# Slots of routed tiles in fewer matmuls, one load of queries moved up, and the last tokens placed by float32 products

## The chip, the core and the metric

The kernel runs on one core of a Trainium2 chip. The metric is the time of one execution in microseconds of device time (us). Five engines work side by side, each through its own instructions in order: TensorE (PE; its weight loads are shown as PEld), VectorE (DVE), ScalarE (ACT), GpSimd (POOL) and SyncE (SP). They wait for each other by semaphores. Most DMA transfers are issued from SP's queue, the scattered and gathered rows from POOL's.

## The reference

Three layers in a row: an attention with a window of 32 and 32 global tokens, a layer of eight experts of which each token takes one, and a dense layer with a fixed curve. Cut to what matters:

```python
s_g = scale * q_g @ k_all.T;  out_g = softmax(s_g) @ v_all            # 32 global queries a head
s_l = concat(scale * q_l @ k_g.T, where(|i-j| <= 32, scale * q_l @ k_l.T, -1e9))
out_l = softmax(s_l) @ concat(v_g, v_l)                               # 512 local queries a head
x = tokens(out)                                                       # 1088 rows of 512

logits = x @ w_gate;  e = argmax(logits)
for i in range(N):                            # in the order of the tokens
    if counts[e[i]] < capacity:
        disp[e[i], counts[e[i]]] = x[i];  counts[e[i]] += 1
y = relu(disp @ w1) @ w2;  x = gate * y[e, pos]

h = x @ w_in;  out = where(h >= 1, h, where(h <= -1, 0, (h + 1)**2 / 4)) @ w_out
```

The shapes are 2 batches, 8 heads, 512 local and 32 global tokens, head size 64; 8 experts of 512 x 1024 and 1024 x 512; a dense layer of 512 x 2048 and 2048 x 512. The capacity given is 288 rows for each expert.

## The kernel before

**Attention.** The order is written out by hand as 16 steps: a step is one batch, one half of its 512 local queries (two tiles of 128) and one pair of heads. `scores` multiplies queries and keys (PE), DVE adds the mask and takes the maxima, `exps` is ACT's, `transp` turns the probabilities (PE), `evac_t` copies them out, `av` multiplies with the values. In the loop over the steps k, `exps(k + 1)` and `scores(k + 2)` come first, then what the table `first[k]` holds, then `transp(k)`, `evac_t(k)`, `av(k - 1)`, and then what `plan[k]` holds. The tables hold the global queries (`glob1`, `glob1b`, `glob2`, `glob3`, for four heads at a time, starting at steps 0, 3, 5 and 8), the filling with zeros of the expert buffers `xd` in DRAM, and the routing. From step 2 the weights of expert 0 are loaded too (`raw`), rounded by ACT (`H`, line 218), and their remainder is taken by POOL (`L`, line 230).

**Queries of the global tokens.** `load_unit(u)` and `load_values(u)` issue the loads of keys, queries and values of a pair of heads on SP; for every second u `load_values` also issues the load of four heads' global queries, `QG[u // 2]`, tile `qgt`. `glob1(6)`, in step 8, reads the last of them.

**Routing.** `route(k, b, tp)` is called for three groups of tiles: three tiles of batch 0 (steps 7 to 9), two (10 to 12), three tiles of batch 1 (13 to 15); the last two tiles, (1, 3) and (1, 4), follow behind the loop. For a group, `logits` and `choose` find the expert of each token as a one-hot tile `OH`. `slots` finds where each token goes: with matmuls of 8 columns it adds the experts' base addresses (`base_b`), the counts so far (`racc`), the counts of earlier tiles of the group (`ones_b`) and those of earlier tokens of the same tile (`tri_b`) in `pc`; DVE picks the token's own column (`ex`, `sidx`) and brings `racc` up to date. `x_rows` turns the attention output into rows of tokens (`px` on PE, `xr` on DVE, or on ACT for the 32 global tokens), and `scatter` writes them into `xd` with a DMA from POOL.

**Hand-over.** The first 128 rows of expert 0 are not read back once all tokens are in DRAM. `xt0` is loaded when the third tile of batch 1, (1, 2), has been scattered (line 714). The tokens of the two last tiles are added on PE: `place` (line 725) is a one-hot tile that says to which of the 128 rows each of their tokens goes, and `px0` sums `xt0` by the identity and the last tokens' rows by `place`. In before the last rows are split into two parts of a rounded type, `late0h`, `late1h` (ACT, line 723) and `late0l`, `late1l` (DVE, line 729), so that there are five groups of four matmuls. ACT and DVE then round `px0` into `X0` (lines 743 and 744), with which the first expert starts (line 842).

**Warming.** `keep_warm(n)` issues n matmuls of zeros, which nobody reads: 9 at the start, and 5, 3 and 2 around the hand-over.

**Experts and dense layer.** Eight experts follow, while ACT and DVE round the next weights; then the dense layer, in four groups of columns, over three chunks of tokens.

Of the kernel before, what the change touches and what calls it, by code (L numbers as in the profile page):

```python
# [8 lines left out]
F32 = mybir.dt.float32  # L9
F32R = mybir.dt.float32r  # L10
BF16 = mybir.dt.bfloat16
# [3 lines left out]
ALU = mybir.AluOpType  # L15
AX = mybir.AxisListType
ENG = mybir.EngineType

P = 128
WARM_0, WARM_1, WARM_2, WARM_3, WARM_4 = 9, 5, 3, 2, 0  # L20
WIN = 224


# [5 lines left out]
def tile_attention_moe_ffn(  # L29
# [23 lines left out]
    nc = tc.nc  # L53
    w_in, w_out = w_in.bitcast(U32), w_out.bitcast(U32)
    B, NHP = qd.shape[0], qd.shape[1]
    SL = qd.shape[3]
    EXT = kd.shape[3]
    SG = qg.shape[3] // 4
    D = 64
    S = SL + SG  # L60
    DM, NT = out.shape
    E, _, F = w1.shape
    DFF = w_out.shape[0]
    KD = DM // P
# [62 lines left out]
    def load_values(u):  # L127
        b, hp = divmod(u, NHP)
        VT[u] = at.tile([P, 5, P], F32, tag="vt", name=f"vt{u}", bufs=NBU)
        nc.sync.dma_start(VT[u], vx[b, hp])  # L130
        if hp % 2 == 1:
            QG[u // 2] = at.tile([P, 4 * SG], F32, tag="qgt", name=f"qgt{u}", bufs=4)
            nc.sync.dma_start(QG[u // 2], qg[b, hp // 2])

    mask_sb = at.tile([P, NLT, WIN], F32, name="mask_sb")
    load_unit(0, 0)
# [303 lines left out]
    def tile_rows(i):  # L440
        return SG if i == 0 else P
# [98 lines left out]
    def slots(b, lo, hi):  # L540

        pc = ps_v(f"pc{b}{lo}")
        n = hi - lo
        for i in range(lo, hi):
            o = pc[:, E * (i - lo):E * (i - lo + 1)]
            r = tile_rows(i)
            nc.tensor.matmul(o, ones_b[:1], base_b[:1], start=True, stop=False)
            nc.tensor.matmul(o, ones_b, racc, start=False, stop=False)
            for j in range(lo, i):
                nc.tensor.matmul(o, ones_b[:tile_rows(j)], OH[b][:tile_rows(j), j, :], start=False, stop=False)  # L550
            nc.tensor.matmul(o, tri_b[:r], OH[b][:r, i, :], start=False, stop=True)
        ts = slice(b * NB_ + lo, b * NB_ + hi)
        ex = rt.tile([P, NB_, E], F32, tag="ex", name=f"ex{b}{lo}", bufs=1)
        nc.vector.tensor_tensor(
            out=ex[:, :n, :], in0=pc[:, :E * n].rearrange("p (i e) -> p i e", e=E), in1=OH[b][:, lo:hi, :],
            op=ALU.mult)
        rs = rt.tile([P, E], F32, tag="rs", name=f"rs{b}{lo}", bufs=1)
        nc.vector.tensor_reduce(out=rs, in_=OH[b][:, lo:hi, :].rearrange("p i e -> p e i"), op=ALU.add, axis=AX.X)
        with nc.allow_low_precision(reason="whole numbers, one of the terms not zero"):
            nc.vector.tensor_reduce(out=sidx[:, ts], in_=ex[:, :n, :], op=ALU.add, axis=AX.X)  # L560
        nc.vector.tensor_tensor(out=racc, in0=racc, in1=rs, op=ALU.add)

    def scatter(b, i):
# [59 lines left out]
            nc.sync.dma_start(yd[0:1, :], zero[:1, :])  # L623


    def keep_warm(n):
        warm = ps_a("warm")
        for _ in range(n):
            nc.tensor.matmul(warm, zero.bitcast(BF16)[:, :P], zero.bitcast(BF16)[:, :512], start=True, stop=True)

    keep_warm(WARM_0)
    scores(0)
    exps(0)
    scores(1)
# [6 lines left out]
    load_values(4)  # L641
    load_unit(5)
    load_values(5)
    wq = [(u, c) for u in range(2) for c in range(4)]
    wn = 0

# [12 lines left out]
    def route(k, b, tp):  # L659

        lo, hi = (0, 3) if tp == 0 else (3, 5)
        i = 2 * tp + 1
        x = [lambda j=j: x_rows(b, j) for j in range(lo, hi)]
        sc = [lambda j=j: scatter(b, j) for j in range(lo, hi)]
        first[k] += [lambda: logits(b, i, 2), lambda: recips(b, i, i + 2)]
        plan[k] += [lambda: logits_t(b, i, 2)]
        if tp == 0:
            first[k].append(lambda: logits(b, 0, 1))
            plan[k].append(lambda: logits_t(b, 0, 1))
        plan[k] += [lambda: choose(b, lo, hi)]  # L670
        first[k + 1] += x[:1]
        plan[k + 1] += [lambda: slots(b, lo, hi)] + x[1:2] + sc[:1]
        plan[k + 2] += x[2:] + sc[1:]

    route(7, 0, 0)
    route(10, 0, 1)
# [41 lines left out]
    keep_warm(WARM_1)  # L718
    slots(1, 3, NB_)
    late = [XR[1, 3], XR[1, 4]]  # L720
    halves = [[rt.tile([P, DM], F32R, name=f"late{i}{n}") for n in "hl"] for i in range(2)]
    for (xa, _), x in zip(halves, late):
        nc.scalar.copy(xa, x)
    place = rt.tile([P, 2, P], F32R, name="place")
    nc.vector.tensor_tensor(
        out=place, in0=iota_sb.unsqueeze(1).to_broadcast([P, 2, P]),
        in1=sidx[:, ntile - 2:].unsqueeze(2).to_broadcast([P, 2, P]), op=ALU.is_equal)
    for (xa, xb), x in zip(halves, late):
        nc.vector.tensor_tensor(out=xb, in0=x, in1=xa.bitcast(F32), op=ALU.subtract)
    px0 = ps_t("px0")  # L730
    keep_warm(WARM_2)
    parts = [(halves[i][0], place[:, i, :]) for i in range(2)] + [(xt0, ident)]
    parts += [(halves[i][1], place[:, i, :]) for i in range(2)]
    for ns, k0 in ((range(5), range(KD)),):
        for n in ns:
            x, at_ = parts[n]
            for k in k0:
                ks = slice(k * P, (k + 1) * P)
                nc.tensor.matmul(px0[:, ks], x[:, ks], at_, start=n == k == 0, stop=n == 4 and k == KD - 1)
    keep_warm(WARM_3)  # L740
    v = px0.rearrange("p (k t) -> p k t", k=KD)
    for k0 in (slice(0, 2), slice(2, 4)):
# [668 lines left out]
```

## Time and profile before

| | |
|---|---|
| median of 3 runs | 465.1 us (462.73 to 465.33) |
| profiled execution, its own time | 462.71 us |
| its span | 460.8 us |
| granted clock of TensorE, mean | 1.00 |
| busy: PE, DVE, ACT, POOL | 442.3, 335.2, 242.9, 95.8 us |

The span is the time from the first to the last instruction of the profiled execution; 1.9 us lie around it. Times of single instructions are from that execution, which is 2.4 us below the median. In a timeline the number in brackets is how long the engine had been idle before the row, and what ended it.

### The profile page before, as it was taken

How to read it: one execution, taken by the hardware profiler on the slowest of the kernel's cores; microseconds unless marked ns; L12 is line 12 of the kernel's file. 1: busy time of each engine (PE TensorE's matmuls, PEld its weight loads, DVE VectorE, ACT ScalarE, POOL GpSimd, SP SyncE). 2: the span in 40 equal slices, each digit the busy share in tenths (PEclk: the TensorE clock that was granted, in tenths of full speed). 3: DMA queues.
4: the chain of work that ended last, by engine and by line, in shares of the span. 5: the costliest groups of instructions: out<-in, count | busy, mean ns of one | idle time of the engine just before them, and what ended most of it. 6: DMA issues, size and time to landing. Idle time of an engine off the chain costs nothing. (4 is left out here: it accounts for less than half of the span.)

```text
span 460.8 us, 8110 instructions
## 1 busy us (share of the span) xinstructions
PE 442.3 (96%) x2875; PEld 372.1 (81%) x2876; DVE 335.2 (73%) x715; ACT 242.9 (53%) x508; POOL 95.8 (21%) x98
## 2 busy tenths in 40 slices
PE   8998989999999999999999899998999999999997
PEld 4876677787577777777777799998999899999996
DVE  4787798674156389936898976787888988878633
ACT  5779666273244478726766675645444344534321
POOL 1105365300000000000001642232133131322321
PEclk9999999999999999999999999999999999999999
DMA  8999554589349169963986340653221410000203
GB/s 273 312 332 366 171 185 134 192 278 395 129 127 316 47 242 389 375 239 123 341 299 243 98 149 0 211 200 93 91 75 64 134 49 1 0 2 0 70 1 127
DMA packets 34595, 79.17 MB, mean 172 GB/s; under 512 B 3761, under 2 KB 8497, under 8 KB 34546
## 3 DMA queue, kind: packets, MB, share of 16 engines
q1 hardware_dynamic: 31698, 70.40, 44.8%
q0 software_dynamic: 1408, 4.46, 2.9%
q10 hardware_dynamic: 1440, 3.67, 2.3%
q8 instruction: 29, 0.48, 0.5%
q14 instruction: 20, 0.16, 0.1%
HBM read 63.77 MB, written 14.75 MB: 170 GB/s over the span
## 5 line engine op out<-in xcount | busy, mean ns | idle before, releaser
L1158 PE MATMUL fh<-oldH,H 128*128 128x256 f32 (+1 forms) x256 | 64.7, 328 | 2.6 <-DVE g L1176 2.1
L230 DVE TENSOR_TENSOR L<-raw,H 128x1024 fp32r<-128x1024 f32 x56 | 66.3, 1217 | 0.9 <-ACT H L218 0.6
L1198 PE MATMUL acc<-oldH,H 128*128 128x256 f32 (+2 forms) x240 | 65.1, 332 | 1.3 <-ACT H L280 0.7
L218 ACT CAST H<-raw 128x1024 fp32r<-128x1024 f32 x57 | 58.0, 1049 | 10.0 <-PEq L895 8.2
L1158 PEld LDWEIGHTS fh<-oldH,H 128*128 128x128 f32 x256 | 44.8, 189 | 6.0 <-DVE g L1176 2.5
L1184 ACT CAST oldH<-g 128x256 fp32r<-128x256 f32 (+2 forms) x36 | 17.9, 496 | 56.8 <-DVE g L1176 56.8
L1198 PE MATMUL acc<-oldH,L 128*128 128x256 f32 (+2 forms) x144 | 47.2, 328 | 0.0
L1198 PEld LDWEIGHTS acc<-oldH,H 128*128 128x128 f32 x240 | 43.3, 189 | 4.0 <-issue 1.0
L1172 DVE SCALAR_TENSOR_TENSOR r<-r 128x256 f32<-128x256 f32 (+2 forms) x48 | 31.2, 650 | 21.0 <-ACT r L1163 21.0
L1185 POOL TENSOR_TENSOR oldH<-g,oldH 128x256 fp32r<-128x256 f32 (+2 forms) x24 | 26.8, 1119 | 73.3 <-ACT oldH L1184 63.5
L1158 PE MATMUL fh<-oldH,L 128*128 128x448 f32 (+1 forms) x128 | 41.6, 325 | 0.0
L599 DVE TENSOR_TENSOR hl<-pt,hh 128x512 fp32r<-128x512 f32 (+1 forms) x24 | 15.7, 653 | 35.6 <-ACT hh L598 35.6
L860 PE MATMUL py<-H,hh 128*128 128x512 f32 (+1 forms) x96 | 38.6, 402 | 0.0
L860 PE MATMUL py<-L,hh 128*128 128x512 f32 (+1 forms) x96 | 37.6, 391 | 0.0
L285 DVE TENSOR_TENSOR L<-co,H 128x512 fp32r<-128x512 f32 x32 | 22.9, 722 | 18.4 <-ACT H L280 18.4
L1163 ACT ACTIVATE r<-fh,half 128x256 f32<-128x256 f32 (+2 forms) x48 | 27.0, 564 | 17.5 <-PE fh L1158 17.1
L845 ACT ACTIVATE hs<-ph 128x512 f32<-128x512 f32 (+1 forms) x24 | 14.4, 598 | 41.2 <-PE ph L842 41.0
L1158 PE MATMUL fh<-oldL,H 128*128 128x384 f32 x128 | 35.2, 339 | 0.2
L931 POOL DMA_INDIRECT yg_own<-yd,idx x2 | 2.3, 1135 | 147.5 <-DVE co L270 147.2
L270 DVE SCALAR_TENSOR_TENSOR co<-raw,ca 128x512 uint32<-128x512 uint32 x32 | 31.5, 992 | 0.9
L324 ACT ACTIVATE sm<-sm,ng 128x224 f32<-128x224 f32 x64 | 30.0, 476 | 3.7 <-DVE ng L313 3.7
L860 PE MATMUL py<-H,hl 128*128 128x512 f32 (+1 forms) x96 | 28.5, 401 | 0.0
(202 smaller groups left out, 1014.8 us busy)
## 6 DMA issues: line engine op xcount, KB each, us to landing
raw<-in_w_dram SPq DMA_DIRECT2D x64, 512.0 KB, 5.7
raw<-in_w_in_dram SPq DMA_DIRECT2D x14, 512.0 KB, 4.9
raw<-in_w_out_dram SPq DMA_DIRECT2D x12, 512.0 KB, 3.7
xd<-zero SPq DMA_DIRECT2D x16, 256.0 KB, 5.9
vt<-in_vx_dram SPq DMA_DIRECT2D x8, 320.0 KB, 4.8
xt<-xd SPq DMA_DIRECT2D x8, 256.0 KB, 6.5
yd<-zero SPq DMA_DIRECT2D x8, 256.0 KB, 3.7
yd<-ys SPq DMA_DIRECT2D x8, 256.0 KB, 5.6
```

Of the source, the lines that this page charges most:

```text
L218: nc.scalar.copy(dst, src)
L230: eng.tensor_tensor(out=L[:, sl], in0=RAW.pop((u, c)), in1=H[:, sl].bitcast(F32), op=ALU.subtract)
L270: nc.vector.scalar_tensor_tensor(out=o, in0=lo, scalar=29, in1=a, op0=ALU.logical_shift_right, op1=ALU.bitwise_or)
L285: nc.vector.tensor_tensor(out=L[:, sl], in0=CV.pop((g, c)), in1=H[:, sl].bitcast(F32), op=ALU.subtract)
L324: nc.scalar.activation(SM[s][:, c, :], SM[s][:, c, :], AF.Exp, bias=NG[s][:, c:c + 1], scale=-1.0, accum_out=SUM[b][:, i, col:col + 1])
L860: nc.tensor.matmul(py[:rows], h[:, 4 * q + k, :rows], w[:, 4 * q + k, :], start=q == i == 0, stop=q == 1 and i == len(terms) - 1)
L1158: nc.tensor.matmul(ph[:, :n], w[:, k, :], XC[c][i // 2][:, k, :], start=n_ == 0, stop=n_ == len(terms) - 1)
L1163: nc.scalar.activation(RS[f % 2][:, :n], ph[:, :n], AF.Relu, bias=half, scale=0.5)
L1172: nc.vector.scalar_tensor_tensor(out=r[:, :n], in0=r[:, :n], scalar=1.0, in1=r[:, :n], op0=ALU.min, op1=ALU.mult)
L1184: nc.scalar.copy(gh[:, :n], gt[:, :n])
L1185: nc.gpsimd.tensor_tensor(out=gl[:, :n], in0=gt[:, :n], in1=gh[:, :n].bitcast(F32), op=ALU.subtract)
L1198: nc.tensor.matmul(a[:, :n], p[:, ds], q, start=f == 0 and i == 0, stop=f == nfl - 1 and i == 2)
```

## The change

Six edits.

1. `slots` makes one matmul for all tiles of a group where it made one for each: for three tiles 5 matmuls of 8 to 24 columns where there were 12, for two tiles 4 where there were 7. The update of `racc` becomes a function of its own, `counted`, behind `sidx`.
2. `load_queries(3)` is issued beside the loads of unit 5, ahead of the zero fills, and no longer with unit 7.
3. In the third group of tiles, `scatter` of the tiles and `x_rows` of the third tile come earlier: the third tile's rows are turned ahead of `transp(15)`.
4. The last tokens' rows go into `px0` by float32 products with a float32 `place`: three groups of four matmuls where there were five, `xt0` first; the split on ACT and DVE is gone.
5. `place` comes ahead of the update of `racc`.
6. The matmuls of zeros: 31 of 160 columns at the start where there were 9 of 512, and 1 ahead of `px0` where there were 3.

```diff
-WARM_0, WARM_1, WARM_2, WARM_3, WARM_4 = 9, 5, 3, 2, 0
+WARM_0, WARM_1, WARM_2, WARM_3, WARM_4 = 31, 5, 1, 2, 0
...
-        if hp % 2 == 1:
-            QG[u // 2] = at.tile([P, 4 * SG], F32, tag="qgt", name=f"qgt{u}", bufs=4)
-            nc.sync.dma_start(QG[u // 2], qg[b, hp // 2])
+        if hp % 2 == 1 and u // 2 not in QG:
+            load_queries(u // 2)
...
-        for i in range(lo, hi):
-            o = pc[:, E * (i - lo):E * (i - lo + 1)]
-            r = tile_rows(i)
-            nc.tensor.matmul(o, ones_b[:1], base_b[:1], start=True, stop=False)
-            nc.tensor.matmul(o, ones_b, racc, start=False, stop=False)
-            for j in range(lo, i):
-                nc.tensor.matmul(o, ones_b[:tile_rows(j)], OH[b][:tile_rows(j), j, :], start=False, stop=False)
-            nc.tensor.matmul(o, tri_b[:r], OH[b][:r, i, :], start=False, stop=True)
+        o = pc[:, :E * n].rearrange("p (i e) -> p i e", e=E)
+        nc.tensor.matmul(o, ones_b[:1], base_b[:1].unsqueeze(1).to_broadcast([1, n, E]), start=True, stop=False)
+        nc.tensor.matmul(o, ones_b, racc.unsqueeze(1).to_broadcast([P, n, E]), start=False, stop=False)
+
+        for j in range(1, n):
+            nc.tensor.matmul(o[:, j:], ones_b, OH[b][:, lo + j - 1:lo + j, :].to_broadcast([P, n - j, E]),
+                             start=False, stop=False)
+        nc.tensor.matmul(o, tri_b, OH[b][:, lo:hi, :], start=False, stop=True)
...
-    keep_warm(WARM_0)
+    keep_warm(WARM_0, 160)
...
     load_values(5)
+    load_queries(3)
...
-        plan[k + 1] += [lambda: slots(b, lo, hi)] + x[1:2] + sc[:1]
-        plan[k + 2] += x[2:] + sc[1:]
+        plan[k + 1] += [lambda: slots(b, lo, hi), lambda: counted(b, lo, hi)]
+        if k + 2 < NS - 1:
+            plan[k + 1] += x[1:2] + sc[:1]
+            plan[k + 2] += x[2:] + sc[1:]
+        else:
+
+            plan[k + 1] += sc[:1] + x[1:2] + sc[1:2]
+            first[k + 2] += x[2:] + sc[2:]
...
-    halves = [[rt.tile([P, DM], F32R, name=f"late{i}{n}") for n in "hl"] for i in range(2)]
-    for (xa, _), x in zip(halves, late):
-        nc.scalar.copy(xa, x)
-    place = rt.tile([P, 2, P], F32R, name="place")
+    place = rt.tile([P, 2, P], F32, name="place")
...
-    for (xa, xb), x in zip(halves, late):
-        nc.vector.tensor_tensor(out=xb, in0=x, in1=xa.bitcast(F32), op=ALU.subtract)
+    counted(1, 3, NB_)
     px0 = ps_t("px0")
     keep_warm(WARM_2)
-    parts = [(halves[i][0], place[:, i, :]) for i in range(2)] + [(xt0, ident)]
-    parts += [(halves[i][1], place[:, i, :]) for i in range(2)]
...
+    for n, (x, at_) in enumerate([(xt0, ident), (late[0], place[:, 0, :]), (late[1], place[:, 1, :])]):
+        for k in range(KD):
+            ks = slice(k * P, (k + 1) * P)
+            nc.tensor.matmul(px0[:, ks], x[:, ks], at_, start=n == k == 0, stop=n == 2 and k == KD - 1)
```

SP's queue, before, at the two places where global queries (`qgt`) are loaded; `kr`, `qr`, `vt` are the keys, queries and values of a pair of heads, `xd<-zero` the zero fills:

```order
L130 DMA vt_240<-in_vx_dram 128x640
L133 DMA qgt_242<-in_qg_dram 128x128
L621 DMA xd<-zero 128x512 x2
...
L125 DMA qr_654<-in_qd_dram 128x512
L130 DMA vt_657<-in_vx_dram 128x640
L133 DMA qgt_659<-in_qg_dram 128x128
L205 DMA raw_0_661<-in_w_dram 128x2x512
```

and after, at the first of them:

```order
L130 DMA vt_262<-in_vx_dram 128x640
L136 DMA qgt_264<-in_qg_dram 128x128
L136 DMA qgt_266<-in_qg_dram 128x128
L626 DMA xd<-zero 128x512 x2
L626 DMA xd<-zero 32x512
```

The last load of queries has moved from behind the loads of unit 7 to ahead of the zero fills.

DVE in steps 14 and 15, before (`ex`, `rs`, `sidx`, `racc` belong to the third group's slots, `xr` to the rows of tiles (1, 1) and (1, 2), `pT` and `xT` to the attention):

```order
L554 TENSOR_TENSOR ex_1257<-pc_1244,oh_151 128x24
L558 TENSOR_REDUCE rs_1259<-oh_151 128x8
L560 TENSOR_REDUCE sidx<-ex_1257 128x3
L561 TENSOR_TENSOR racc<-racc,rs_1259 128x8
L501 TENSOR_TENSOR xr_1268<-px_1263,ssum_665 128x512
L339 COPY pT_1283<-tb_1278 96x512
L356 COPY xT_896<-pv_1286 128x256
L501 TENSOR_TENSOR xr_1301<-px_1296,ssum_665 128x512
```

and after:

```order
L557 TENSOR_TENSOR ex_1262<-pc_1256,oh_151 128x24
L561 TENSOR_REDUCE sidx<-ex_1262 128x3
L565 TENSOR_REDUCE rs_1265<-oh_151 128x8
L566 TENSOR_TENSOR racc<-racc,rs_1265 128x8
L504 TENSOR_TENSOR xr_1276<-px_1271,ssum_687 128x512
L504 TENSOR_TENSOR xr_1286<-px_1281,ssum_687 128x512
L342 COPY pT_1301<-tb_1296 96x512
L359 COPY xT_911<-pv_1304 128x256
```

The third tile's rows have moved ahead of the two attention copies.

PE at the hand-over, before, from the last slots' end to the end of `px0`:

```order
L551 MATMUL pc_1370<-oh_151,tri_b 128x8
L629 LDWEIGHTS zero
L629 MATMUL warm<-zero 128x512
...
L739 MATMUL px_1394<-place,late0h 128x128 x4
L739 MATMUL px_1394<-place,late1h 128x128 x4
L739 MATMUL px_1394<-ident,xt_1352 128x128 x4
L739 MATMUL px_1394<-place,late0l 128x128 x4
L739 MATMUL px_1394<-place,late1l 128x128 x4
```

and after:

```order
L554 MATMUL pc_1375<-oh_151,tri_b 128x16
L634 LDWEIGHTS zero
L634 MATMUL warm<-zero 128x512
L745 MATMUL px_1388<-ident,xt_1357 128x128 x4
L745 MATMUL px_1388<-place,xr_1335 128x128 x4
L745 MATMUL px_1388<-place,xr_1337 128x128 x4
```

The product of `xt0` has moved from the third place to the first, and the two products of each last tile have become one.

## Rows read from the trace of the kernel before

**Rows 1.** The page: busy time by engine, and the chain that ended last.

```profile
PE 442.3 (96%) x2875; PEld 372.1 (81%) x2876; DVE 335.2 (73%) x715; ACT 242.9 (53%) x508; POOL 95.8 (21%) x98
...
PE 27%; DVE 13%; ACT 4%; issue 1%; DVEq 0%; ACTq 0%
```

**Rows 2.** Windows: stretch, length, busy by engine, granted clock, DMA share, GB/s.

```profile
20.00:40.00 20.00, 20.00 (x283) 15.47 (x281) 14.45 (x60) 14.88 (x54) 4.05 (x2) 1.00 1.02 343
...
92.00:110.00 18.00, 17.72 (x87) 13.97 (x86) 12.70 (x16) 10.72 (x16) 0.99 (x2) 1.00 0.89 319
```

**Rows 3.** Timeline of the start: start, length, what, idle before and releaser.

```profile
1.31 3.88 PE L629 MATMUL warm<-zero 128*128 128x512 bf16 x9 [1.31 <-POOL zero L142]
...
4.27 0.15 PEld L629 LDWEIGHTS <-zero 128*128 128x128 bf16 x1 [0.28 <-issue]
...
5.12 1.91 PE L308 MATMUL sp<-kr,qr 64*128 64x224 f32 x16
...
10.17 1.36 PE L367 MATMUL g<-kr,qgt 64*32 64x288 f32 x16 [0.61 <-DMA qgt<-in_qg_dram]
...
11.46 0.68 PEld L308 LDWEIGHTS sp<-kr,qr 64*128 64x128 f32 x8 [0.41 <-DMA qr<-in_qd_dram]
```

**Rows 4.** Timeline: ACT waits for weights, PE waits for DVE.

```profile
32.64 1.05 ACT L218 CAST H<-raw 128x1024 fp32r<-128x1024 f32 x1 [1.60 <-DMA raw<-in_w_dram]
...
42.87 0.71 PEld L308 LDWEIGHTS sp<-kr,qr 64*128 64x128 f32 x8 [2.13 <-DVE m L532]
```

**Rows 5.** Timeline of step 8: the last global queries and the first slots.

```profile
46.21 1.67 PE L419 MATMUL gpv<-gT,vt 128*64 128x32 f32 x40
...
48.82 1.12 PE L367 MATMUL g<-kr,qgt 64*32 64x288 f32 x16 [0.94 <-DMA qgt<-in_qg_dram]
...
49.87 0.17 PE L547 MATMUL pc<-base_b,ones_b 1*128 1x8 bf16 x1
...
50.65 0.15 DVE L375 TENSOR_SCALAR gs<-gs 128x1 f32<-128x1 f32 x1
...
50.94 0.64 PE L487 MATMUL px<-ident,xT 128*128 128x128 f32 x4
...
51.12 0.18 DVE L554 TENSOR_TENSOR ex<-pc,oh 128x24 f32<-128x24 f32 x1 [0.32 <-PE pc L551]
```

**Rows 6.** DMA issues of 41.3 to 41.9 us: KB each, us to landing; unit 7's keys.

```profile
kr<-in_kd_dram SPq DMA_DIRECT2D x1, 304.0 KB, 5.4
```

**Rows 7.** Timeline: SP issues those keys; POOL and DVE in step 9.

```profile
41.58 0.42 SPq L124 DMA_DIRECT2D kr<-in_kd_dram  x1
...
53.55 2.37 POOL L230 TENSOR_TENSOR L<-raw,H 128x1024 fp32r<-128x1024 f32 x1
...
54.98 0.97 DVE L388 SCALAR_TENSOR_TENSOR gs<-gs 128x1 f32<-128x1 f32 x1
```

**Rows 8.** Timeline of POOL in steps 14 and 15: the third group's scatters.

```profile
79.51 0.88 POOL L566 DMA_INDIRECT xd<-xr,sidx  x1 [5.07 <-DVE xr L501]
80.70 0.99 POOL L566 DMA_INDIRECT xd<-xr,sidx  x1 [0.30 <-DVE pT L339]
82.29 0.97 POOL L566 DMA_INDIRECT xd<-xr,sidx  x1 [0.60 <-DVE ssum L507]
```

**Rows 9.** Line 566 in 86 to 88 us: durations in ns, first and last start.

```profile
L566 POOLq EVENT_SEMAPHORE  x1: 43/43/43, 87.8 to 87.8; - x1
```

**Rows 10.** Timeline of the hand-over.

```profile
85.02 0.33 SPq L714 DMA_DIRECT2D xt<-xd  x1
...
87.29 0.42 DVE L725 TENSOR_TENSOR place<-iota_sb,sidx 128x256 fp32r<-128x256 f32 x1
...
87.86 0.63 PE L739 MATMUL px<-place,late0h 128*128 128x128 f32 x4 [0.38 <-ACT late1h L723]
...
88.78 1.11 PE L739 MATMUL px<-ident,xt 128*128 128x128 f32 x8
...
89.64 0.64 PE L739 MATMUL px<-place,late0l 128*128 128x128 f32 x4
...
90.76 0.65 ACT L743 CAST x0h<-px 128x256 fp32r<-128x256 f32 x2 [2.95 <-PE px L739]
```

More of the change, by code (lines that the diff above doesn't have):

```diff
@@ L130, in load_values, with load_queries @@
         nc.sync.dma_start(VT[u], vx[b, hp])
-        if hp % 2 == 1:
-            QG[u // 2] = at.tile([P, 4 * SG], F32, tag="qgt", name=f"qgt{u}", bufs=4)
-            nc.sync.dma_start(QG[u // 2], qg[b, hp // 2])
+        if hp % 2 == 1 and u // 2 not in QG:
+            load_queries(u // 2)
+    def load_queries(g):
+        QG[g] = at.tile([P, 4 * SG], F32, tag="qgt", name=f"qgt{g}", bufs=4)
+        nc.sync.dma_start(QG[g], qg[divmod(2 * g, NHP)[0], 2 * g % NHP // 2])
     mask_sb = at.tile([P, NLT, WIN], F32, name="mask_sb")
@@ L556, in slots, with counted @@
             op=ALU.mult)
+        with nc.allow_low_precision(reason="whole numbers, one of the terms not zero"):
+            nc.vector.tensor_reduce(out=sidx[:, ts], in_=ex[:, :n, :], op=ALU.add, axis=AX.X)
+    def counted(b, lo, hi):
         rs = rt.tile([P, E], F32, tag="rs", name=f"rs{b}{lo}", bufs=1)
         nc.vector.tensor_reduce(out=rs, in_=OH[b][:, lo:hi, :].rearrange("p i e -> p e i"), op=ALU.add, axis=AX.X)
-        with nc.allow_low_precision(reason="whole numbers, one of the terms not zero"):
-            nc.vector.tensor_reduce(out=sidx[:, ts], in_=ex[:, :n, :], op=ALU.add, axis=AX.X)
         nc.vector.tensor_tensor(out=racc, in0=racc, in1=rs, op=ALU.add)
@@ L623, in zero_fill, with keep_warm @@
             nc.sync.dma_start(yd[0:1, :], zero[:1, :])
-    def keep_warm(n):
+    def keep_warm(n, cols=512):
         warm = ps_a("warm")
         for _ in range(n):
-            nc.tensor.matmul(warm, zero.bitcast(BF16)[:, :P], zero.bitcast(BF16)[:, :512], start=True, stop=True)
-    keep_warm(WARM_0)
+            nc.tensor.matmul(warm[:, :cols], zero.bitcast(BF16)[:, :P], zero.bitcast(BF16)[:, :cols], start=True,
+                             stop=True)
+    keep_warm(WARM_0, 160)
     scores(0)
@@ L727, in tile_attention_moe_ffn @@
         in1=sidx[:, ntile - 2:].unsqueeze(2).to_broadcast([P, 2, P]), op=ALU.is_equal)
-    for (xa, xb), x in zip(halves, late):
-        nc.vector.tensor_tensor(out=xb, in0=x, in1=xa.bitcast(F32), op=ALU.subtract)
+    counted(1, 3, NB_)
     px0 = ps_t("px0")
     keep_warm(WARM_2)
-    parts = [(halves[i][0], place[:, i, :]) for i in range(2)] + [(xt0, ident)]
-    parts += [(halves[i][1], place[:, i, :]) for i in range(2)]
[L734 to L739, printed above, removed]
+    for n, (x, at_) in enumerate([(xt0, ident), (late[0], place[:, 0, :]), (late[1], place[:, 1, :])]):
+        for k in range(KD):
+            ks = slice(k * P, (k + 1) * P)
+            nc.tensor.matmul(px0[:, ks], x[:, ks], at_, start=n == k == 0, stop=n == 2 and k == KD - 1)
     keep_warm(WARM_3)
```

## The prediction

> **What bounds the kernel now.** I read the page first: PE is busy for 96% of the span, DVE for 73%, and the chain that ended last lies on PE for 27% and on DVE for 13% of the span [rows 1]. That chain reaches back only into the dense layer, which the change does not touch, so I asked which stretches hand an earlier end on. The windows say it: in the first stretch of the experts PE works 17.72 of 18 us, and the granted clock is at full speed [rows 2]. So what the change gains or loses ahead of the first expert should reach the end nearly unchanged, unless a transfer with a time of its own stands in between. In the attention three engines hand work round, and PE's busy share says little there (20.00 of 20 us, but with modelled ends); there I read PE's waits one by one. Four matter: at the start PE waits for loads twice [rows 3]; in step 7 it waits 2.13 us for DVE [rows 4]; in step 8 0.94 us for the last global queries [rows 5]; and the hand-over to the experts is a chain of its own [rows 8 to 10].
>
> **The start: 31 short matmuls for 9 long ones.** The nine begin at 1.31 and the first scores at 5.12, one matmul every 0.427 us, which is 512 columns at 1.2 GHz [rows 3]. The new ones have 31 x 160 = 4960 columns against 4608; if their weight loads stay hidden, at the same clock they take 31 x 0.133 = 4.13 us and end at 5.44, or somewhat earlier where the clock rises, so the scores come 0.1 to 0.3 us later. If a pair is bound by its load of 0.15 us [rows 3], they end at 1.31 + 31 x 0.15 = 5.96, 0.8 us later. Below zero the edit cannot go by more than the 0.1 us between the last warm-up matmul and the scores. I take 0 for the end of the kernel, because a cover lies behind it: at 10.17 PE had been idle for 0.61 us waiting for the first global queries, and at 11.46 the weight side 0.41 us for a load of queries [rows 3]. Those loads are issued by SP whatever PE does. Without the cover, the cost is the 0.1 to 0.8.
>
> **The queries' load moved up.** In step 8 `gpv` ends at about 47.88, and `g` starts at 48.82 after 0.94 us of waiting for `qgt` [rows 5]. What is late next? The same matmuls read unit 7's keys. These were issued at 41.58 [rows 7] and took 5.4 us [rows 6], so they were there at 46.98, ahead of 47.88. The whole 0.94 us go. The load costs elsewhere: 64 KB are put ahead of the zero fills and the first weights in SP's queue, at a time when DMA runs at 343 GB/s [rows 2], which is 0.19 us of delay for all behind it. One of these, the first weight chunk, is waited for by ACT for 1.60 us [rows 4], and ACT's rounding then sets POOL and DVE in step 7. I count the 0.19 as a loss; its ends are 0 and the 0.43 us that SP takes for an issue (as SP's 0.42 us for the keys [rows 7]).
>
> **Slots in fewer matmuls.** The twelve of step 8 start at 49.87, and what follows them starts at 50.94 [rows 5]: 1.07 us, 0.09 each. Five should take 0.45, so PE has 0.62 us more. DVE can use only part: `ex` had waited 0.32 us for PE [rows 5], and ahead of it stands `glob1`'s small arithmetic up to 50.80, so DVE and all that follows `sidx` gain 0.3. Which of the two reaches the end? In step 9 POOL's `L` runs from 53.55 to 55.92, and DVE's L388, an operation on one column, lasts 0.97 us, from 54.98 to 55.95: it ended with POOL's [rows 7]. POOL's order puts that `L` behind the scatter that waits for `sidx`, so the stall moves with DVE's 0.3 and not with PE's 0.6. I take 0.3; the ends are 0 and 0.62. The Trainium skill (SBUF — State Buffer, on the port pair that DVE and GpSimd share) says that the pair is locked for a whole instruction and the other engine fully blocks. By that rule PE's larger gain is lost at this stall, and the sum holds 0.3; without it, it would hold 0.6. The row agrees with the rule. In the second group seven become four: 3 x 0.09 = 0.27 at most, 0 at least; I take 0.2. The third group's gain is in the next part.
>
> **The hand-over.** Before, the five groups of four in `px0` start at 87.83 and their result is taken at 90.76. A group of rounded operands takes about 0.45 (87.86 to the next, and 89.64 on), the float32 group of `xt0`, shown as eight passes, 0.86 to 0.89 (88.78 to 89.64) [rows 10]. So 4 x 0.45 + 0.89 = 2.69 before, and 3 x 0.89 = 2.67 after: PE's own work is the same, and what changes is when it may start. Before, that was set by ACT's second cast, behind `place` (87.29 + 0.42 = 87.71) [rows 10]. After, `xt0` comes first. When did it land? POOL's wait for its landing was over at 87.8 [rows 9], 5.5 us after the start of the third scatter at 82.29 [rows 8], since SP may load `xt0` only when that scatter has landed (issue at 85.02 [rows 10]). After, the third scatter's rows come right behind the second's, and `sidx` 0.2 us earlier (7 x 0.09 = 0.63 less on PE, of which DVE, busy with two copies ahead of `ex`, can use about 0.2); then POOL's spacing of 1.2 us [rows 8] bounds it: 79.3, 80.5, 81.7. So `xt0` lands 0.6 us earlier, at 87.2, and `px0` is done 87.83 - 87.2 = 0.6 us earlier. `place` is not late: it is needed only at 87.2 + 0.89, and it was there at 87.71 even before. The two casts, the two subtractions and two matmuls of zeros go at no gain of their own: PE waits for `xt0` at that place. The ends: 0, if the scatter does not move, and 1.8, if `xt0` is never waited for. In that case `place` is the bound, 0.8 earlier at 86.9 (0.6 from PE, 0.2 from two small operations fewer ahead of it, each 0.15 at most, as L375 [rows 5]), and two groups and the 0.2 us to the result follow: 86.9 + 1.78 + 0.2 = 88.9 against 90.76. The scatters of the last two tiles stand behind `xt0` on POOL and move with it; SP's next loads of weights and of the second expert's rows move with them.
>
> **Sum.** 0 + 0.19 - 0.94 - 0.3 - 0.2 - 0.6 = -1.85 us. The profiled execution took 462.71 us, so it would be 460.9. Of the runs shown two were near 465.2 and one at 462.73; the median, 465.1, is 2.4 above the profiled one. Against the median the forecast is 463.3 us.
>
> **Rivals.**
> (a) `xt0` is early and `place` the bound. For it: POOL had waited 5.07 us when it started the first scatter, and 0.60 ahead of the third [rows 8], so it has time to spare. Against it: POOL's spacing. Hand-over -1.8 for -0.6: 465.1 - 3.05 = 462.05, say 462.0.
> (b) The gain of step 8 does not last: between step 9 and step 14 the chains of ACT and POOL, which hold the weights of expert 0, set the pace, and what PE and DVE gain is taken back by such a wait. For it: the stall in rows 7, and PE's 2.13 us in rows 4, which show that PE is not the bound everywhere. Against it: POOL's chain there begins at `sidx`, and so moves too. Then only the hand-over is left: 0.19 - 0.6 = -0.4, 464.7.
> (c) Slower: the short matmuls of the start. If a weight load and its matmul do not overlap, a pair takes 0.15 [rows 3] + 0.133 = 0.283, 31 of them 8.8 us, and the scores start at 10.1, 5.0 later. The covers of 0.61 and 0.41 [rows 3] take off 1.0, ACT's 1.60 [rows 4] at most 1.6 more; 2.4 are left, less 1.85: +0.5, or 465.6. It decides from a pair of 0.27 us on. Against it: with 512 columns the pace was exactly that of the columns, so the load was hidden. The Trainium skill (TensorE: Matmul & The Clock Gate, on what overlaps) says that a weight load overlaps running matmuls only where the rows of the array differ, and puts a load at columns / 1.2, which is 0.107 us by that page; its pair would take 0.24 and its kernel stay 0.8 us ahead of the median, an estimate. The trace does not agree, since the nine loads were hidden.
> (d) The change does nothing that lasts: 465.1.
>
> **Chances.** The forecast 0.5, (a) 0.17, (b) 0.15, (c) 0.08, (d) 0.1. The range: unknown ends of the forecast run from -3.6 (0.94 + 0.62 + 0.27 + 1.8) to about 0, which gives 461.5 to 465.1; the level of the runs adds its own, since a median that falls on the level of the profiled execution would lie 2.4 lower, at 460.9 for the forecast and 459.7 for (a), and on the upper side (c) and (d) reach 465.6. I take 459.8 to 465.9. A difference of 1% (4.65 us) is about what a measurement of this kernel can tell from none. Faster by more needs a time below 460.45: the forecast or (a) together with the lower level, 0.2. Slower by more needs 469.8, which none of the cases reaches by itself: 0.05. Within 1%: 0.75.
>
> **What would show it.** In the changed profile: PE's wait for `qgt` in step 8 gone and `g` directly behind `gpv`; four to five small matmuls in each slots; the third scatter 1.2 us behind the second; `xt0`'s eight passes ahead of both products with `place`, started by the load and not by DVE; the first matmul of `ph` about 1.85 us earlier than 91.3. Wrong would be the forecast if `px0` starts before `xt0` has been waited for, if steps 9 to 13 end no earlier than before, if the first scores start after 6 us and PE no longer waits at 10.17, or if the experts, from 92 us on, meet a wait for weights that takes the gain back.

## The result: 467.4 us against 465.1, a little slower

The changed kernel takes 467.39 us (median of 9 runs, 464.06 to 470.06), the kernel before in the same comparison 465.1 (9 runs, 462.73 to 465.78). The ratio is 1.0057, with a 95% interval of 1.0032 to 1.0083: half a per cent, and not much more than the 0.3% by which the kernel before will differ from itself below. The forecast was 463.3 us; the time lies above its range of 459.8 to 465.9. The profiled execution of the changed kernel took 468.04 us, with a span of 466.3 and a mean granted clock of 0.989, where the one of before took 462.71 at 1.0. So the two profiles stand 5.3 us apart, and the medians 2.3: part of what the profiles show is not the change. Two runs of those told below were slow as a whole, one of the kernel before (483.79) and one of the last experiment (467.34), and the ratios leave them out.

At the start both of the forecast's covers are there. The timeline of the changed kernel's start (start, length, engine, line, operation, tiles; in brackets the idle time before and what ended it) answers to [rows 3]:

```profile
1.31 4.26 PE L634 MATMUL warm<-zero 128*128 128x160 bf16 x31 [1.31 <-POOL zero L145]
5.50 1.15 PE L311 MATMUL sp<-kr,qr 64*128 64x224 f32 x8
...
10.44 1.28 PE L370 MATMUL g<-kr,qgt 64*32 64x288 f32 x16 [0.49 <-DMA qgt<-in_qg_dram]
...
11.64 0.68 PEld L311 LDWEIGHTS sp<-kr,qr 64*128 64x128 f32 x8 [0.41 <-DMA qr<-in_qd_dram]
```

In these two profiles the 31 short matmuls ended 0.38 us later than the nine long ones. Both waits for loads behind them are still there, and the second ended 0.18 us later (11.64 for 11.46): they cover half of the delay. The same matmuls vary by as much: over all profiles of this case the 31 took 3.61 to 4.32 us and the nine 3.68 to 4.02.

The timeline of steps 7 and 8 answers to [rows 4, 5]:

```profile
33.57 1.04 ACT L221 CAST H<-raw 128x1024 fp32r<-128x1024 f32 x1 [2.27 <-DMA raw<-in_w_dram]
...
43.56 1.86 PE L311 MATMUL sp<-kr,qr 64*128 64x224 f32 x8 [1.81 <-DVE m L535]
...
49.78 1.66 PE L422 MATMUL gpv<-gT,vt 128*64 128x32 f32 x40
51.38 1.12 PE L370 MATMUL g<-kr,qgt 64*32 64x288 f32 x16
52.43 0.18 PE L548 MATMUL pc<-base_b,ones_b 1*128 1x24 bf16 x1
...
52.66 0.64 PE L490 MATMUL px<-ident,xT 128*128 128x128 f32 x4
...
53.29 0.17 DVE L557 TENSOR_TENSOR ex<-pc,oh 128x24 f32<-128x24 f32 x1
```

Two steps of the forecast are there: `g` follows `gpv` with no wait for the queries, and the slots take 0.23 us (52.43 to 52.66) where they took 1.07. But `g` starts 2.56 us later than before. The windows of the same stretch (length, busy time of PE, PEld, DVE, ACT and POOL, granted clock, DMA share, GB/s) show why:

```profile
42.00:44.00 2.00, 0.44 (x2) 0.47 (x4) 1.97 (x14) 2.00 (x7) 0.87 (x1) 0.73 0.99 306
44.00:46.00 2.00, 2.00 (x12) 1.25 (x11) 1.97 (x7) 0.93 (x4) 1.48 (x1) 0.50 1.00 381
...
48.00:50.00 2.00, 2.00 (x27) 1.98 (x26) 0.69 (x2) 0.00 (x0) 0.00 (x0) 0.56 1.04 400
```

The same place in the kernel before, `sp` and a window (PE's own idle time was 1.88 us; the 2.13 of [rows 4] is the weight side's):

```profile
42.90 1.03 PE L308 MATMUL sp<-kr,qr 64*128 64x224 f32 x8 [1.88 <-DVE m L532]
...
44.00:46.00 2.00, 2.00 (x26) 1.79 (x26) 2.00 (x10) 1.28 (x4) 0.79 (x1) 1.00 0.99 341
```

In the changed kernel PE idled for 1.81 us, then ran at a granted clock of 0.50, which is 1.2 GHz, and was back at full speed only from 50 us on. From the start of `sp` to the start of `g` it took 7.82 us, against 4.98 from `sp` to the end of `gpv` before, so 2.84 us were lost. The first experiment will show that the kernel before does this too.

The next loss is the change's own. Here are the timelines of step 10, of the changed kernel first. The instruction on `ssum` adds 1e-9 to the sums of the exponentials, `L<-raw,H` is GpSimd's share of rounding the experts' weights, and `H<-raw` the cast by ACT that each such product needs:

```profile
60.62 4.81 DVE L510 TENSOR_SCALAR ssum<-ssum 128x16 f32<-128x16 f32 x1
...
60.73 4.65 POOL L233 TENSOR_TENSOR L<-raw,H 128x1024 fp32r<-128x1024 f32 x2
...
61.57 1.05 ACT L221 CAST H<-raw 128x1024 fp32r<-128x1024 f32 x1
...
66.63 0.97 PE L490 MATMUL px<-ident,xT 128*128 128x128 f32 x4 [4.29 <-DVE xT L359]
```

The same instructions of the kernel before:

```profile
58.45 2.53 DVE L507 TENSOR_SCALAR ssum<-ssum 128x16 f32<-128x16 f32 x1
...
58.57 4.78 POOL L230 TENSOR_TENSOR L<-raw,H 128x1024 fp32r<-128x1024 f32 x2
...
59.86 1.05 ACT L218 CAST H<-raw 128x1024 fp32r<-128x1024 f32 x1
...
62.20 0.65 PE L487 MATMUL px<-ident,xT 128*128 128x128 f32 x4 [1.57 <-DVE xT L356]
```

An addition on 16 columns lasts 4.81 us and ends with GpSimd's two products. Before, it lasted 2.53 and ended at 60.98, at the seam of the two (58.57 plus half of 4.78 is 60.96). What differs is the cast that the second product needs. Before, it ended at 60.91, as the first product did, so that the second began with a gap and, as I read it, DVE got in. After, it ended at 62.62, with the first product still running until 63.05; the second followed at once. PE waits 4.29 us for what DVE does behind the addition, before 1.57. Behind that wait the clock falls once more:

```profile
64.00:66.00 2.00, 0.00 (x0) 0.00 (x0) 1.97 (x3) 0.48 (x3) 1.38 (x1) 1.00 0.90 233
66.00:68.00 2.00, 1.37 (x7) 1.37 (x8) 1.93 (x11) 0.00 (x0) 0.00 (x0) 0.71 0.82 193
68.00:70.00 2.00, 2.00 (x15) 1.61 (x15) 1.97 (x11) 0.58 (x1) 0.00 (x0) 0.50 0.24 98
```

At the next `px`, behind the second group's slots, the changed kernel is 5.80 us late. The timeline of its hand-over answers to [rows 8, 10]:

```profile
85.11 0.87 POOL L571 DMA_INDIRECT xd<-xr,sidx  x1 [4.84 <-DVE racc L566]
86.28 0.99 POOL L571 DMA_INDIRECT xd<-xr,sidx  x1 [0.30 <-issue]
87.58 0.97 POOL L571 DMA_INDIRECT xd<-xr,sidx  x1 [0.30 <-issue]
...
90.31 0.33 SPq L728 DMA_DIRECT2D xt<-xd  x1
...
92.41 0.42 DVE L736 TENSOR_TENSOR place<-iota_sb,sidx 128x256 f32<-128x256 f32 x1
...
92.99 1.16 PE L745 MATMUL px<-ident,xt 128*128 128x128 f32 x8 [1.07 <-DMA xt<-xd]
...
95.98 0.65 ACT L749 CAST x0h<-px 128x256 fp32r<-128x256 f32 x2 [10.58 <-PE px L745]
```

The three scatters stand 2.47 us from first to last (before 2.78), PE waits for `xt0` and not for `place`, and `x0h` starts 5.22 us later than before. From 5.80 to 5.22 the last steps and the hand-over gave back 0.58 us; the forecast was 0.6.

### The profile page after: what moved, and what is told of

Read it like the earlier page. It is cut to its first block, busy times and chain, and to the rows that moved or that the text cites. A ratio compares the mean times of both kernels' runs of the same rounds, so it can differ in the third digit from the quotient of the medians.

```text
span 466.3 us, 8107 instructions
## 1 busy us (share of the span) xinstructions
PE 444.9 (95%) x2876; PEld 376.7 (81%) x2876; DVE 337.4 (72%) x713; ACT 241.6 (52%) x506; POOL 94.8 (20%) x98
```

## The experiments

After the first comparison I had four accounts of the loss. A: DVE's addition is held by two GpSimd products in a row, because the slots' gain brings ACT's cast forward, and the clock falls behind the idle. B: the moved load makes the weights late. C: DVE is late for some other reason (each expectation below says which). D: the start.

**The kernel before once more.** No edit.

> The kernel before, once more, for the granted clock and the span of each of its runs; the profiled run of before had 1.0 throughout and 462.71 us, its median is 465.1. Theory A (the loss of the changed kernel is a DVE operation held by GpSimd at the second recips, and TensorE idle that lets the clock fall to 1.2 GHz): the kernel before has runs without a fall near 462.7 and runs with one short fall near 465, with mean clocks of about 1.0 and 0.99. Rival B (the loss is late data from the moved load, the clock has no part in it): the clock is 1.0 in all runs of before, whatever their times.

Measured: 466.64 us (10 runs), against 465.05 for the kernel before in the same comparison (31 runs); ratio 1.003, 1.0003 to 1.0058. The two are the same program, so a difference of 0.3% means nothing here, even where the interval leaves out 1. Its ten clocks lie between 0.988 and 0.996, so B's "1.0 in all runs" falls. Two windows of its profile, and ACT's first cast of weights:

```profile
42.00:44.00 2.00, 0.54 (x3) 0.56 (x5) 1.97 (x15) 2.00 (x7) 0.93 (x1) 0.71 1.02 398
44.00:46.00 2.00, 2.00 (x12) 1.26 (x9) 1.97 (x5) 0.86 (x4) 1.42 (x1) 0.50 1.05 393
...
33.51 1.04 ACT L218 CAST H<-raw 128x1024 fp32r<-128x1024 f32 x1 [3.02 <-DMA raw<-in_w_dram]
```

The first fall of the clock and the late first cast (33.51, in the changed kernel 33.57, in the profile of before 32.64) both occur in the kernel before. Neither needs the change. The first profile of before, at a clock of 1.0, was one of its faster runs. Its addition in step 10 lasted 2.54 us here. And `g` started at 51.27 with no wait for the queries: behind the fall PE was so late that the load in its old place was in time.

**The addition left out of the changed kernel.**

```diff
         sv = SUM[b][:, lo - 1:hi - 1, :]
-        nc.vector.tensor_scalar_add(sv, sv, 1e-9)
         nc.vector.reciprocal(sv, sv)
```

> The changed kernel without the addition of 1e-9 to the sums in recips (sums of at least 1, which the addition doesn't change in float32), so that the instruction that lasted 4.81 us at 60.62 isn't there. Theory A: the reciprocal behind it, which had no such stall in either trace, is done by about 61, px of step 10 comes 3 to 4 us earlier, the second fall of the clock goes, and the time falls by 3 to 5 us, to 463 to 464.5; the first fall, in step 7, stays. Rival B (late data): 467 as the changed kernel. Rival C (the reciprocal is held in its place by the same two GpSimd operations): 467 too, with 4 to 5 us on the reciprocal's row.

Measured: 461.86 us, ratio to before 0.9936 (0.9907 to 0.9965): 5.5 us less than the changed kernel, more than expected. In its profile the clock did not fall in step 7, but from 64 to 70 us, the other way round than expected. The reciprocal takes 0.25 us. The wait did not go altogether; it moved to the next instruction that takes both its inputs from SBUF, the write of the one-hot rows:

```profile
61.09 2.28 DVE L538 TENSOR_TENSOR oh<-iota_sb,i 128x16 bf16<-128x16 f32 x1
```

It ends at 63.37 with GpSimd's second product (58.63 + 4.70 = 63.33). C as this run's expectation has it, the reciprocal held in the addition's place, falls: what waits is a later instruction, and only for the second product.

**The load put back**, the rest as changed.

```diff
     load_unit(5)
     load_values(5)
-    load_queries(3)
```

> The changed kernel with the last queries' load back behind the last unit's loads; slots, hand-over and start stay as changed. Rival B (late data from the moved load is the cause): the first raw weights land 0.9 us earlier, ACT's first cast at 32.6 in place of 33.6, TensorE's sp of step 7 at 42.9, the global matmuls of step 8 wait 0.94 us for the queries again, no long stall of DVE at the second recips, and the time is 464 to 465. Theory A with the load as its only trigger says the same; theory A with the shortened slots as the trigger (0.84 us earlier at step 8, which moves the recips against GpSimd's casts) says 466 to 468 with the stall of 4 to 5 us still there.

Measured: 467.49 us, ratio 1.0049 (1.0019 to 1.008). The wait for the queries is back, the first cast is at 32.30, and the long addition is there:

```profile
48.10 1.12 PE L370 MATMUL g<-kr,qgt 64*32 64x288 f32 x16 [1.82 <-DMA qgt<-in_qg_dram]
...
57.33 4.82 DVE L510 TENSOR_SCALAR ssum<-ssum 128x16 f32<-128x16 f32 x1
```

B falls: without the moved load the loss is the same. The load's wait added nothing to the time, and the profiles show a likely reason. Of the six with the load in its old place, three have the wait and no fall of the clock in step 7 (before 0.94 us, this one 1.82, the kernel before without the collision 1.48), and three have the fall and no wait (the kernel before once more, without its addition, with the slots). The moved load can only save a wait that is there. How often each case comes up in runs without a profile is not known.

**Nine long matmuls at the start again**, the rest as changed.

```diff
-    keep_warm(WARM_0, 160)
+    keep_warm(WARM_0)
```

`WARM_0` is 9 again.

> The changed kernel with the start's nine matmuls of 512 columns again in place of 31 of 160. Rival D (the start, 0.38 us later at the first scores, is what moves everything): first scores at 5.1, ACT's first cast of weights earlier by 0.3 to 0.4 us, and 464 to 466. Theories A and B: the loads at 10 and 11.5 us cover the start, the rest stays, 467 to 468.

Measured: 466.52 us, ratio 1.0049 (1.0014 to 1.0084).

```profile
55.77 4.83 DVE L510 TENSOR_SCALAR ssum<-ssum 128x16 f32<-128x16 f32 x1
```

First scores at 4.92, `g` behind its load at 10.03. The time lies half a microsecond above what D expected and as much below A's, so it doesn't tell them apart alone; but the long addition is there without the short matmuls, so the start doesn't cause it.

**The addition left out of the kernel before.** The same edit as above.

> The kernel before without the addition of 1e-9 to the sums (which are at least 1, so that nothing changes in float32). Theory A: of the 5.6 us that the same edit gave the changed kernel, the kernel before gets little at the second recips, since it lost 2.53 us there and not 4.81, and the one-hot write a few instructions later (2.28 us in the changed kernel without the addition) is held in its place by GpSimd's second product: that write ends at about 63.4 in place of 63.6 us, and the time is 464 to 465. Rival E (the addition costs its own wait wherever it stands): the 2.53 and 1.86 us both come back, 460.5 to 462.

Measured: 463.7 us, ratio 0.9965 (0.9942 to 0.9987), 0.3 us below what A expected. 1.4 us in the kernel before, and 5.5 in the changed one, for one and the same instruction: what it costs depends on what stands beside it. The one-hot write is held here as well:

```profile
61.61 2.32 DVE L535 TENSOR_TENSOR oh<-iota_sb,i 128x16 bf16<-128x16 f32 x1
```

The expectation's E, that the addition costs its own wait wherever it stands, would have 460.5 to 462 and falls.

**Only the slots**, in the kernel before.

```diff
-        for i in range(lo, hi):
-            o = pc[:, E * (i - lo):E * (i - lo + 1)]
...
+        o = pc[:, :E * n].rearrange("p (i e) -> p i e", e=E)
...
+        nc.tensor.matmul(o, tri_b, OH[b][:, lo:hi, :], start=False, stop=True)
```

> The kernel before with the slots of several tiles in fewer matmuls, and nothing else of the change. Theory A (TensorE comes 0.84 us earlier out of step 8, ACT's cast is then done before GpSimd ends its first product, its two products follow without a gap, and DVE's addition waits for both): 4.8 us on that addition, 7.9 us between GpSimd's second product and the next scatter, 466 to 468. Rival F (the moved load or the hand-over brings the collision): 2.53 us and 4.1 us as before, and 464 to 465.

Measured: 465.89 us (461.98 to 468.44), ratio 0.9999 (0.9962 to 1.0037). Its profile has the collision:

```profile
58.49 4.83 DVE L507 TENSOR_SCALAR ssum<-ssum 128x16 f32<-128x16 f32 x1
...
64.53 1.12 PE L487 MATMUL px<-ident,xT 128*128 128x128 f32 x4 [4.32 <-DVE xT L356]
```

and 7.62 us between GpSimd's second product and the next scatter, before 4.11. So the slots alone bring it, and F, by which the load or the hand-over does, falls. That they alone make the kernel slower is not shown: the ratio is 1, the median lies just below what A expected and above F's 464 to 465, and the runs spread over 6.5 us. Whether each of them had the collision isn't seen.

**Only the first group's slots undone**, in the changed kernel.

```diff
+        if b == 0 and lo == 0:
+            for i in range(lo, hi):
+                o1 = pc[:, E * (i - lo):E * (i - lo + 1)]
...
+        else:
+            nc.tensor.matmul(o, ones_b[:1], base_b[:1].unsqueeze(1).to_broadcast([1, n, E]), start=True, stop=False)
```

> The changed kernel with the first group's slots in twelve matmuls again; the other groups' slots, the moved load, the start and the hand-over stay as changed. Theory A: TensorE is 0.84 us later at the end of step 8, the addition waits 2.5 us and not 4.8, 4.1 us between GpSimd's second product and the next scatter, 463.5 to 465. Rival F (the moved load brings the collision, by the wait that it takes away in step 8): 4.8 us still, 467.

Measured: 463.53 us, ratio 0.9978 (0.995 to 1.0006), clocks of 0.996 to 1.0. With twelve matmuls in place of five the kernel is 3.9 us faster than the changed one:

```profile
57.87 2.52 DVE L510 TENSOR_SCALAR ssum<-ssum 128x16 f32<-128x16 f32 x1
...
61.61 0.66 PE L490 MATMUL px<-ident,xT 128*128 128x128 f32 x4 [1.57 <-DVE xT L359]
```

The addition and PE's wait are those of the kernel before, and the moved load, the start and the hand-over stay in. F would have 467 and falls again. Together with the run before this is the core of the case: in the changed kernel, the 0.84 us saved on PE in step 8 are what costs.

A rival remains for the size: this profile has no fall of the clock in step 7 either, which lies ahead of the edit, so the 3.9 us need not be the slots' alone. The stretch behind step 7 settles it. From `g` to the second group's slots PE took 17.4 us in the three profiles with a short addition (both of the kernel before, and this one) and 20.6 to 20.9 in the four with a long one (the changed kernel, the load put back, the long start, the slots alone), whether the clock had fallen in step 7 or not. The slots' gain taken off, the collision costs 3.2 to 3.5 us there. In the same profiles the cast had ended about 0.05 us before the first product in the three, and 0.34 to 0.43 in the four. No run moves the cast alone; that it is the cast which decides is read from these rows.

**GpSimd's product of step 10 one step later**, in the changed kernel, and the three behind it too.

```diff
             weight_h(*wq[c], nc.scalar)
-            weight_l(*wq[c], nc.gpsimd)
+        c = k - 5 if k < 10 else k - 6
+        if 5 <= k < 14 and k != 10:
+            weight_l(*wq[c], nc.gpsimd)
```

> The changed kernel with GpSimd's product of step 10 put into step 11 and the three after it one step later each, so that no two stand in a row at the second recips; the addition stays. Theory A: the addition waits for one product only (at most 2.5 us), the one-hot write behind it for none, and the time is 462 to 464. Rival C (DVE is late there by itself, the products only happen to run beside it): 467.

Measured: 467.31 us, ratio 1.0027 (1.0005 to 1.0049): the expected 462 to 464 were missed. The collision went from step 10 and came up in step 13, where the shifted products now stand in a row beside the third addition:

```profile
59.09 2.53 DVE L510 TENSOR_SCALAR ssum<-ssum 128x16 f32<-128x16 f32 x1
73.01 4.18 DVE L510 TENSOR_SCALAR ssum<-ssum 128x16 f32<-128x16 f32 x1
...
72.47 4.68 POOL L233 TENSOR_TENSOR L<-raw,H 128x1024 fp32r<-128x1024 f32 x2
```

The expectation had taken in the one place and not the next. The miss bears the mechanism out: two products in a row, 4 to 5 us; one, 2.5.

**The collision taken away**, in the changed kernel and in the kernel before. Both leave out the addition, and make the product of steps 7 and 10 begin behind the one-hot write:

```diff
-        nc.vector.tensor_scalar_add(sv, sv, 1e-9)
...
+            if k in (7, 10):
+                nc.gpsimd.tensor_copy(seen, OH[0][:, 2 if k == 7 else 4, :])
             weight_l(*wq[c], nc.gpsimd)
```

> The changed kernel without the addition of 1e-9 (sums of at least 1), and with a copy of 8 numbers of the one-hot rows on GpSimd ahead of its product in steps 7 and 10, so that the product begins only when DVE has written the one-hot rows. Theory A: no DVE instruction of step 10 lasts over 1 us, the 2.28 us on the one-hot write are gone, GpSimd's second product begins 0.2 to 0.5 us later and holds nobody, and the time falls by another 2 us below the changed kernel without the addition, to 459 to 460.5. Rival C (TensorE or the loads set the pace of these steps, and DVE's waits beside GpSimd are in their shadow): 461.9, as without the addition alone.

> The same two edits on the kernel before, so that the change can be weighed without the collision. Theory A: 461 to 463, and the changed kernel with the same edits is 1 to 2.5 us faster than this one, as the sum of the prediction has it (1.85 us); if the change has a loss of its own besides the collision, the two are equal or the changed one is slower.

Measured: the changed kernel 459.86 us (458.66 to 461.29), ratio to before 0.9877 (0.9847 to 0.9908), its clock 0.999 or 1.0 in all runs; the kernel before 464.21, ratio 0.9981 (0.9961 to 1.0002), clocks of 0.991 to 1.0. The first is the fastest of all versions, by 5.2 us against the kernel before. Its step 10:

```profile
60.93 0.17 DVE L538 TENSOR_TENSOR oh<-iota_sb,i 128x16 bf16<-128x16 f32 x1
...
61.24 0.19 POOL L712 COPY seen<-oh 128x8 bf16<-128x8 bf16 x1 [0.39 <-DVE oh L538]
61.39 2.37 POOL L233 TENSOR_TENSOR L<-raw,H 128x1024 fp32r<-128x1024 f32 x1
```

GpSimd waits 0.39 us, and DVE no longer for microseconds. C as this expectation has it, that PE or the loads set the pace, would have 461.9 and falls. So without the collision the change is worth 4.35 us, more than the 1.85 of the forecast's sum. Both parts of what was expected of the kernel before were missed: it gained less (464.21 for 461 to 463), and the distance is larger than 1 to 2.5 us. Its profile shows what held it up: the wait for the queries in step 8, and the clock behind it.

```profile
49.01 1.12 PE L367 MATMUL g<-kr,qgt 64*32 64x288 f32 x16 [1.48 <-DMA qgt<-in_qg_dram]
...
52.00:54.00 2.00, 2.00 (x10) 1.39 (x11) 0.77 (x2) 0.00 (x0) 1.36 (x2) 0.50 0.07 26
```

**The copy on GpSimd alone**, in the changed kernel, with the addition in place.

> The changed kernel with its addition, and with the copy on GpSimd ahead of its product in steps 7 and 10 as the only edit: one instruction more and nothing less. Theory A: the addition in step 10 waits for one product (2.4 us) and not for two (4.8), and 467.4 becomes 463 to 464.5. Rival E (the addition itself is what costs): 467.

Measured: 465.51 us, ratio 1.0016 (0.9992 to 1.004). The addition lasts 2.54 us, as expected, but the time is 1 us above what was expected: PE still waits 1.96 us behind it, and in the profile the clock falls there, and once more at the hand-over:

```profile
56.41 2.54 DVE L510 TENSOR_SCALAR ssum<-ssum 128x16 f32<-128x16 f32 x1
...
60.00:62.00 2.00, 1.84 (x9) 1.83 (x10) 1.90 (x14) 0.46 (x2) 0.13 (x1) 0.52 0.69 244
...
84.00:86.00 2.00, 1.78 (x8) 1.48 (x9) 1.35 (x9) 0.00 (x0) 0.00 (x0) 0.50 0.44 131
```

The second stands behind a wait of PE for DVE of 0.96 us. The profile with the load put back has the like, and none of the other profiles has a fall there. One instruction more made the kernel some 1.9 us faster, though the two ratios' intervals overlap by a little (from 1.0032 to 1.004). The account that the addition itself costs has 467 and does not allow that.

**The moved load alone**, in the kernel before without the collision.

```diff
     load_unit(5)
     load_values(5)
+    load_queries(3)
```

> The kernel before with the two edits that take the collision away (no addition of 1e-9, GpSimd's copy ahead of its product in steps 7 and 10), and the last queries' load moved up, with none of the other parts of the change. The profiled run without the moved load had TensorE wait 1.5 us for the queries in step 8 and the clock at 1.2 GHz from 51 to 55 us behind that wait; its median was 464.2, and the changed kernel with the same edits had 459.9. Theory G (most of those 4.3 us are the moved load, by the wait of 0.9 to 1.5 us and by the clock that no longer falls behind it): 461 to 462. Theory H (the load gives its wait alone, the slots and the hand-over the rest): 463 to 463.5.

Measured: 461.64 us (five runs, 460.24 to 462.35), ratio to before 0.9907 (0.9875 to 0.994); without the load it was 0.9981. That is 0.74% or 3.4 us for one load, with some 1.8 us of uncertainty, where the wait itself was 0.9 to 1.5. That is G's 461 to 462 and not H's.

```profile
44.00:46.00 2.00, 2.00 (x12) 1.72 (x11) 1.33 (x8) 1.43 (x5) 2.00 (x1) 0.50 1.05 409
...
49.04 1.12 PE L370 MATMUL g<-kr,qgt 64*32 64x288 f32 x16
```

`g` starts with no wait, and no window behind it has a clock below 1.0 until 92 us. But ahead of it the clock had fallen in step 7, and behind such a fall the old place of the load had no wait either. So the load's worth rests on the times here, of two comparisons on two chips, and not on this profile. What the other parts of the change add, 0.9877 against 0.9907, is 1.4 us and no larger than the uncertainty.

## Why the prediction was wrong

The step that failed is in the part on the slots: "the stall moves with DVE's 0.3 and not with PE's 0.6. I take 0.3". The two gains were rightly told apart. From `g` to `px` the changed kernel took 0.84 us less than before, from `g` to `ex` 0.39. But I let the rest of PE's gain end at the stall at no cost. The 0.45 us by which PE got further ahead than DVE went to ACT: its copy of `gta` and its cast behind it came 0.45 us earlier against GpSimd's products (the cast ended 0.43 us before the first product did, and before 0.05). That closed the gap in which DVE had got in. The addition went from 2.53 to 4.81 us, PE's wait from 1.57 to 4.29, and the clock fell behind it, which made the stretch from `px` to the second group's slots 5.60 us long (66.63 to 72.23) where it had been 3.98 (62.20 to 66.18). By PE's rows that is -0.84 in step 8, then +2.72 of waiting and +1.62 at the low clock: the stretch from `g` to the second group's slots became 3.5 us longer, where the sum has -0.3. The profiles of the other runs have 3.2 to 3.5 for it, and by the times 3.9 us went with the first group's slots undone. The clock behind a longer wait was a cost that the sum had at nothing. The prediction's own sign of being wrong, "if steps 9 to 13 end no earlier than before", came true.

The Trainium skill (SBUF — State Buffer, section "SBUF: two separate sides") calls the port pair that DVE and GpSimd share an exclusive lock, held for a whole instruction. I cited it for the wrong conclusion. The trace agrees for the addition, which ended at 65.43 with the products at 65.38, and adds what decided here: of two products in a row DVE got in between only where the second had to wait for its input, 2.53 us against 4.81.

Rival (b) named the right place, steps 9 to 14, and the wrong sign: it had the gain taken back, not turned into a loss. Rival (c), the slower one, named the start by weight loads that are not hidden, 8.8 us for the 31; they took 4.26.

Point by point. The start: 0.18 us of its delay came through in the two profiles, for the forecast's 0, and the times with the long start don't tell it from nothing. The queries' load: its wait is gone, also in four profiles of variants in which the clock had not fallen in step 7 (the long start, the old slots, no collision, the copy alone); a fifth, without the addition, waited 0.58 us there for unit 7's keys, which the forecast had in time. But -0.94 fits neither kernel. In the changed kernel the load put back cost nothing that the times show (467.49 for 467.39); without the collision the load was worth 3.4 of 464, where one profile without it has the clock falling behind the wait, which the sum left out. The weights' delay of 0.19: not to be seen, since between two profiles of the kernel before the first cast moves by 0.87 us by itself (32.64 and 33.51). The slots: 0.05 us each, not 0.09; the second group's term of 0.2 was 0.25. The hand-over: -0.58 for -0.6, and with `xt0` as its bound, not `place`, as the sum has it; it is one profile, and two others of the changed kernel have a fall of the clock there. The level: the profile of before had a clock of 1.0, and of 94 runs of that kernel 13 had 0.999 or more, with a median of 463.4 us, the other 81 one of 465.2. So the rows came from the rarer level, which I saw only as a spread of 2.4 us.

## What to carry to other kernels

Where one engine is held by another's long instructions, ask of a gain on a third engine whether it closes a gap in which the held one got through. Look for it before the edit: an instruction on a few columns that lasts microseconds, and ends when the other engine's does, is such a place, and a second one like it can stand a few rows behind, as the one-hot write does here. An idle time of TensorE is priced with the clock behind it; so one profile at full clock is no base when most runs have less.

## What the runs showed of the hardware

What of DVE's work waits for GpSimd depends on the form of the DVE instruction. Beside GpSimd's product an addition of a constant on SBUF (4.81 us) and a comparison of two SBUF operands (2.28) waited for its end; copies out of PSUM, a reduction in SBUF (0.39), MAX8 and FIND_INDEX8 in the same stretch kept their 0.1 to 0.6 us.

TensorE's clock fell to 1.2 GHz behind an idle of about 4.3 us in each of the four profiles that had one there (the changed kernel, the load put back, the long start, the slots alone). Behind 1.8 to 1.9 us in step 7 it fell in the changed kernel and in the second profile of before, but not in the first. The length of the last idle did not decide it: in step 10 the clock fell behind 1.96 us with the copy on GpSimd alone, and not behind 2.01 with the product one step later. The price of one fall, read from the same work at either level, was 1.3 to 1.6 us in step 10 and 2.8 in steps 7 and 8.
